# A two-layer recurrent-memory transformer on one core: the memory value sum in column halves, a shorter memory softmax, and the score scale folded into weight products

## Chip, cores, metric

The kernel runs on one core of one Trainium2 chip. The metric is the device time of one execution in microseconds (us). TensorE (PE) multiplies, with its weight loads shown apart as PEld; VectorE (DVE) and ScalarE (ACT) work on vectors and move results out of PSUM; GpSimd (POOL) copies a little; SyncE (SP) issues transfers.

## What is computed

```python
def A(x, mem0):                       # x: 2048 x 448, mem: 8 x 448, 16 heads of 256
    mem = mem0
    for s in range(64):               # segments of 32 tokens
        h = concat(mem, x[32*s : 32*s+32])            # 40 rows
        q, k, v = h @ Wq, h @ Wk, h @ Wv              # per head
        p = softmax(mask(q @ k.T / 16))               # masked scores are -1e9
        o = (p @ v) @ Wo                              # summed over heads
        mem, out[s] = o[:8], o[8:]                    # memory goes to the next segment
    return out
def B(x):
    return (relu(x @ W_gate) * (x @ W_up)) @ W_down
x = x + A(layernorm(x), mem0); x = x + B(layernorm(x))    # layer 0
x = x + A(layernorm(x), mem0); x = x + B(layernorm(x))    # layer 1, the same weights
```

The memory makes `A` a recurrence: segment s+1 cannot start its scores before the 8 memory rows of segment s are there. The two layers run as a pipeline: layer 1 works four segments behind layer 0, in the same step, so there are 68 steps.

## The kernel before

**Weights.** For each head, `M = Wq Wk^T` and `N = Wv Wo` are formed once at the start (`setup`), so that scores are `h M h^T` and the output is `p (h N)`. Both lie in SBUF in 56 blocks of 128 rows (`NO = 56`), with the last 64 of the 448 rows apart (`M3`).

**A step** (`step`, L1399) handles one segment of each layer. The memory's part comes first and is the recurrence: `t_block` forms `M h` (11 groups, in three blocks, copied out to `TTm` and `TTs`), `s_mem` forms the memory rows' scores and their softmax, `p_t_mem` transposes the probabilities, `u_mem` forms `p h` (copied to `UTm`), `un_mem` multiplies it by `N` and sums over the 56 blocks, `m_t` picks the memory rows and transposes them into the next segment's `hT`, and `m_nat` brings them into `hK` in their natural layout. `s_seg`, `seg_pt`, `u_seg` (four pieces) and `un` do the same for the 32 token rows and are not on the recurrence. `ln_b`, `b_layer` and `b_down` are layer B for two segments at a time.

**The order.** No loop sets the order of the instructions. A planner (`_Order.run`, L388) places all operations, engine by engine, by priorities. The priority of a TensorE group is its due time in the table `SLOT`, whose names end in the step modulo 4, so that the order repeats every four steps; the first and last four steps have entries of their own. `BIAS` shifts the priorities of the operations on other engines; its entry `stay` favours a group that needs no new tiling, and `win` sets how far ahead the planner looks. An operation that may run on ACT or DVE (`cp`, L859) goes where the planner expects it to end first. What comes out is a fixed order on each engine, with semaphore waits between engines.

**TensorE's tilings.** Matmuls use the whole 128\*128 array, or four tiles of 64\*64 side by side, or four tiles of 128 rows by 32 columns. `un_mem` uses the last: four quarters of the 56 blocks run side by side, each with the same 32 rows of `UTm` (of both layers) and all 448 columns, and leave four partial sums on the four quarters of PSUM's partitions.

**The sum of the quarters.** In steps 4 to 63 (`stacked`), ACT copies the lower half of the partitions to `sumA` (L1177), DVE adds the upper half into `sumB` (L1178), ACT rounds it to bf16 in the upper half of `hi` (L1179), and DVE writes the rest, again in bf16, into its lower half (L1180). `m_t` and `m_nat` then multiply `hi` by a constant selection matrix (`selm`, `seln`), which adds all rows that belong together. In the other steps `hi` and `lo` are two whole tiles (L1182, L1183), and `m_t` and `m_nat` run over both.

**The memory softmax** (L1070 to L1076): DVE takes the maximum, DVE subtracts it, ACT takes the exponential with the scale 1/16, DVE sums the rows, DVE takes the reciprocal, DVE multiplies. The scores of both layers lie side by side, 40 columns each.

Of the kernel before, what the change touches and what calls it, by code (L numbers as in the profile page):

```python
# [7 lines left out]
F32 = dt.float32  # L8
# [15 lines left out]
NO = 56  # L24
SCALE = 1.0 / 16.0
NEG = -1.6e10
# [18 lines left out]
class _Sched:  # L45
# [118 lines left out]
    "t_blockm+": -2572, "t_blocks+": 1814, "s_mem+": -72176, "p_t_mem+": -4403, "u_mem+": 20875, "un_mem+": -547,  # L164
    "un_memh+": -38848, "m_t+": 9355, "m_tk+": 2366, "s_seg+": 16120, "seg_pt+": 3438, "u_seg0+": -16088,
    "u_seg1+": -717, "u_seg2+": 13160, "u_seg3+": -691, "m_nat+": 82793, "t_block0f+": 12092, "t_block0r+": 515,
    "t_block1r+": -532, "t_block2r+": -10266, "ln_a+": -5223, "ln_ac+": 1567, "un+": 139105, "ln_b+": -4368,
    "b_layer+": 350, "b_down+": 117514, "stay": 11757, "win": 172,
# [5 lines left out]
    "t_block0f.0@a0": 64557, "t_block0r.0@a0": 48742, "t_block0r.1@a0": 66297, "t_block0r.2@a0": 48724,  # L174
    "t_block0r.3@a0": 47759, "t_block0r.4@a0": 48126, "t_block0r.5@a0": 48733, "t_block1f.0@a0": 45822,
    "t_block1r.0@a0": 82085, "t_block1r.1@a0": 94319, "t_block1r.2@a0": 78536, "t_block1r.3@a0": 97965,
    "t_block2r.0@a0": 94795, "s_mem.0@a0": 47753, "fills_mem.0@a0": 56612, "fills_mem.1@a0": 79507,
    "p_t_mem.0@a0": 82024, "u_mem.0@a0": 84238, "fillu_mem.0@a0": 101473, "un_mem.0@a0": 94797, "m_t.0@a0": 96319,
    "s_seg.0@a0": 93758, "u_seg0.0@a0": 85662, "u_seg1.0@a0": 93046, "u_seg2.0@a0": 84258, "u_seg3.0@a0": 93059,
    "m_nat.0@a1": 102575, "t_block0f.0@a1": 47148, "t_block0r.0@a1": 50336, "t_block0r.1@a1": 50332,  # L180
    "t_block0r.2@a1": 50330, "t_block0r.3@a1": 50334, "t_block0r.4@a1": 50338, "t_block0r.5@a1": 50328,
    "t_block1f.0@a1": 47763, "t_block1r.0@a1": 81935, "t_block1r.1@a1": 93766, "t_block1r.2@a1": 93762,
    "t_block1r.3@a1": 93760, "t_block2r.0@a1": 93764, "s_mem.0@a1": 53687, "fills_mem.0@a1": 53691,
    "fills_mem.1@a1": 50369, "p_t_mem.0@a1": 52961, "u_mem.0@a1": 93157, "fillu_mem.0@a1": 66292,
    "un_mem.0@a1": 95431, "m_t.0@a1": 38530, "s_seg.0@a1": 53689, "u_seg0.0@a1": 93038, "u_seg1.0@a1": 93040,
    "u_seg2.0@a1": 93746, "u_seg3.0@a1": 93044, "un0.0@a1": 126022, "un0.1@a1": 126024, "un0.2@a1": 108479,
    "un0.3@a1": 108070, "un1.0@a1": 109020, "un1.1@a1": 103707, "un1.2@a1": 102591, "un1.3@a1": 126036,
    "un2.0@a1": 125114, "un2.1@a1": 126311, "un2.2@a1": 128901, "un2.3@a1": 126313, "un3.0@a1": 126315,
    "un3.1@a1": 126319, "b_layerf.0@a1": 99747, "b_layer.0@a1": 101458, "b_layer.1@a1": 101460,
    "b_layerf.1@a1": 101451, "b_layer.2@a1": 101464, "b_layer.3@a1": 101524, "b_down.0@a1": 101526,  # L190
    "b_down.1@a1": 101468, "b_down.2@a1": 101460, "b_down.3@a1": 101543, "b_down.4@a1": 100495, "b_down.5@a1": 101459,
    "b_down.6@a1": 101539, "m_nat.0@a2": 81979, "t_block0f.0@a2": 47146, "t_block0r.0@a2": 50203,
    "t_block0r.1@a2": 50211, "t_block0r.2@a2": 50986, "t_block0r.3@a2": 50213, "t_block0r.4@a2": 50205,
    "t_block0r.5@a2": 102340, "t_block1f.0@a2": 47162, "t_block1r.0@a2": 102255, "t_block1r.1@a2": 101373,
    "t_block1r.2@a2": 102257, "t_block1r.3@a2": 103206, "t_block2r.0@a2": 50207, "s_mem.0@a2": 59668,
    "p_t_mem.0@a2": 50201, "u_mem.0@a2": 49539, "un_mem.0@a2": 126026, "m_t.0@a2": 126317, "s_seg.0@a2": 122371,
    "u_seg0.0@a2": 113514, "u_seg1.0@a2": 101453, "u_seg2.0@a2": 101528, "u_seg3.0@a2": 101526, "m_nat.0@a3": 126321,
    "t_block0f.0@a3": 49554, "t_block0r.0@a3": 51471, "t_block0r.1@a3": 59670, "t_block0r.2@a3": 59445,
    "t_block0r.3@a3": 50305, "t_block0r.4@a3": 59668, "t_block0r.5@a3": 53676, "t_block1f.0@a3": 49552,
    "t_block1r.0@a3": 100508, "t_block1r.1@a3": 102247, "t_block1r.2@a3": 57648, "t_block1r.3@a3": 101523,  # L200
    "t_block2r.0@a3": 101638, "s_mem.0@a3": 100835, "p_t_mem.0@a3": 101462, "u_mem.0@a3": 100431,
    "un_mem.0@a3": 102605, "m_t.0@a3": 102609, "s_seg.0@a3": 108012, "u_seg0.0@a3": 102306, "u_seg1.0@a3": 102308,
    "u_seg2.0@a3": 102312, "u_seg3.0@a3": 102310, "un0.0@a3": 102607, "un0.1@a3": 107006, "un0.2@a3": 101455,
    "un0.3@a3": 100684, "un1.0@a3": 128108, "un1.1@a3": 101462, "un1.2@a3": 101527, "un1.3@a3": 101529,
    "un2.0@a3": 101531, "un2.1@a3": 101533, "un2.2@a3": 102308, "un2.3@a3": 102310, "un3.0@a3": 102312,
    "un3.1@a3": 102314, "b_layerf.0@a3": 110205, "b_layer.0@a3": 102298, "b_layer.1@a3": 102300,
    "b_layerf.1@a3": 134704, "b_layer.2@a3": 102093, "b_layer.3@a3": 102302, "b_down.0@a3": 101528,
    "b_down.1@a3": 101530, "b_down.2@a3": 101532, "b_down.3@a3": 128003, "b_down.4@a3": 125876, "b_down.5@a3": 106989,
    "b_down.6@a3": 101460, "m_nat.0@0": 136794, "t_block0f.0@0": 58621, "t_block0r.0@0": -19774,
    "t_block0r.1@0": 1609, "t_block0r.2@0": -19782, "t_block0r.3@0": -19780, "t_block0r.4@0": -19778,  # L210
    "t_block0r.5@0": -19776, "t_block1f.0@0": 43923, "t_block1r.0@0": -26408, "t_block1r.1@0": -26410,
    "t_block1r.2@0": -26406, "t_block1r.3@0": -26404, "t_block2r.0@0": 59598, "s_mem.0@0": -32879,
    "p_t_mem.0@0": -19990, "u_mem.0@0": -22021, "un_mem.0@0": -32867, "m_t.0@0": -214033, "s_seg.0@0": 76854,
    "u_seg0.0@0": -22167, "u_seg1.0@0": 43918, "u_seg2.0@0": 319270, "u_seg3.0@0": -23555, "m_nat.0@1": -115912,
    "t_block0f.0@1": -24982, "t_block0r.0@1": -32859, "t_block0r.1@1": -32863, "t_block0r.2@1": -32861,
    "t_block0r.3@1": -32857, "t_block0r.4@1": -20205, "t_block0r.5@1": -32865, "t_block1f.0@1": -23529,
    "t_block1r.0@1": 53151, "t_block1r.1@1": -32851, "t_block1r.2@1": -32853, "t_block1r.3@1": 53153,
    "t_block2r.0@1": -25980, "s_mem.0@1": 53134, "p_t_mem.0@1": 53139, "u_mem.0@1": 61163, "un_mem.0@1": 233375,
    "m_t.0@1": 151657, "s_seg.0@1": 53145, "u_seg0.0@1": 147020, "u_seg1.0@1": 147022, "u_seg2.0@1": 179549,
    "u_seg3.0@1": 147024, "un0.0@1": 147166, "un0.1@1": 62233, "un0.2@1": -23765, "un0.3@1": 65649, "un1.0@1": 61020,  # L220
    "un1.1@1": 237653, "un1.2@1": 151655, "un1.3@1": 237659, "un2.0@1": 237654, "un2.1@1": 151661, "un2.2@1": 151663,
    "un2.3@1": 151638, "un3.0@1": 144006, "un3.1@1": 148365, "b_layerf.0@1": 129357, "b_layer.0@1": 318027,
    "b_layer.1@1": 67000, "b_layerf.1@1": 215789, "b_layer.2@1": 145588, "b_layer.3@1": 61456, "b_down.0@1": -24827,
    "b_down.1@1": -33972, "b_down.2@1": 319243, "b_down.3@1": 319245, "b_down.4@1": 147237, "b_down.5@1": 61345,
    "b_down.6@1": 239065, "m_nat.0@2": 402948, "t_block0f.0@2": 388846, "t_block0r.0@2": 59139,
    "t_block0r.1@2": -26865, "t_block0r.2@2": -26863, "t_block0r.3@2": -26927, "t_block0r.4@2": 145141,
    "t_block0r.5@2": -26869, "t_block1f.0@2": 179407, "t_block1r.0@2": 293702, "t_block1r.1@2": 311085,
    "t_block1r.2@2": 311131, "t_block1r.3@2": 311131, "t_block2r.0@2": 225148, "s_mem.0@2": -30419,
    "p_t_mem.0@2": 59349, "u_mem.0@2": 179549, "un_mem.0@2": -28407, "m_t.0@2": -115541, "s_seg.0@2": 153276,
    "u_seg0.0@2": 318226, "u_seg1.0@2": 317538, "u_seg2.0@2": 232221, "u_seg3.0@2": 146407, "m_nat.0@3": 141188,  # L230
    "t_block0f.0@3": 60228, "t_block0r.0@3": 141563, "t_block0r.1@3": 55559, "t_block0r.2@3": 55561,
# [301 lines left out]
class _Kernel:  # L533
# [16 lines left out]
    def alloc(self):  # L550
# [33 lines left out]
        self.PTm = self.sb("PTm", [128, 128])  # L584

        self.UTm = self.sb("UTm", [128, NO, 64])
        self.hi = self.sb("hi", [128, D])
        self.lo = self.sb("lo", [128, D])
        self.sumA = self.sb("sumA", [64, D], F32)
        self.sumB = self.sb("sumB", [64, D], F32)  # L590
# [871 lines left out]
```

## Time and profile before

| | |
|---|---|
| median of three runs | 1541.28 us (1539.87 to 1543.81) |
| profiled execution | 1540.8 us |
| ACT, DVE busy | 57%, 60% of the span |
| `sumA` copy, ACT, 64 x 448 | 60 of 540 ns |
| `sumB` add, DVE, 64 x 448 | 60 of 614 ns |
| `hi` rounding, ACT | 60 of 575 ns |
| `hi` rest, DVE | 60 of 702 ns |
| softmax maximum, subtraction, sum (DVE, 128 x 80) | 60 each of 238, 241, 231 ns |
| softmax exponential (ACT, 128 x 80) | 60 of 269 ns |

How to read it: the page lists busy times by engine, then the chain of work that ended last, then groups of instructions. A group's row has its line, engine and operation, what it writes and reads, the tile of the array (128\*32), the shape, the number of instructions, their busy time in us and mean in ns, and, after the bar, the idle time of the engine just before them and who ended it. A row of the timeline has the start in us, the duration in us, the engine, the operation, and how many instructions were merged. All matmuls have the line L138, that of a helper, so they are told apart by their tiles: `Nw,UTm` is `un_mem`, `selm` is `m_t`, `seln` is `m_nat`, `PTm,hK` is `u_mem`, `PTs,hK` is `u_seg`, `ident,Pm` is `p_t_mem`, `hT,M` and `hT,Mw` are `t_block`, `Nw,big` is `un`, `xBT,big` and `big,hB` are layer B.

### The profile page before, as it was taken

What the parts mean: (1) busy time and instruction counts of PE and PEld (TensorE: products, weight loads), DVE (VectorE), ACT (ScalarE), POOL (GpSimd) and SP (SyncE); (2) the same over time, 40 slices, a digit from 0 to 9 for tenths busy, and PEclk for the clock granted to TensorE, in tenths of its full rate; (3) what the DMA queues carried; (4) which work ended last, traced back from release to release, by engine and by line L of the source; (5) the groups of instructions that cost most, each with busy time, mean ns of one, the idle gap of its engine ahead of it and who ended that gap; (6) DMA issues with size and microseconds to landing.
All of it is one profiled execution on the core that took longest, in us unless ns stands there. A gap on an engine that the chain in (4) does not pass through costs nothing.

```text
span 1540.8 us, 79677 instructions
## 1 busy us (share of the span) xinstructions
PE 1478.4 (96%) x36772; PEld 1084.9 (70%) x36777; DVE 919.9 (60%) x2445; ACT 882.9 (57%) x2627; POOL 111.8 (7%) x259
## 2 busy tenths in 40 slices
PE   5999989999999999999999999999999999999998
PEld 2567666777676776777677777767677677767675
DVE  7555556656565656655665665656565665566555
ACT  5635555656656565565656565565566566565543
POOL 4000000000000000000000000000000000000000
PEclk9999999999999999999999999999999999999999
DMA  9840100000000000000000010000000010000000
GB/s 224 184 129 16 22 10 20 20 15 17 20 20 15 21 16 19 16 16 20 16 20 15 22 18 15 17 20 20 15 21 16 20 19 16 15 15 19 18 19 14
DMA packets 129726, 45.86 MB, mean 30 GB/s; under 512 B 117736, under 2 KB 129264, under 8 KB 129392
## 3 DMA queue, kind: packets, MB, share of 16 engines
q1 hardware_dynamic: 129040, 40.53, 12.3%
q8 instruction: 288, 4.72, 1.3%
q14 instruction: 46, 0.38, 0.1%
q10 hardware_dynamic: 352, 0.24, 0.1%
HBM read 10.33 MB, written 1.84 MB: 8 GB/s over the span
## 4 chain that ended last, share of the span: by engine, by line
PE 87%; DVE 6%; ACT 4%; DMA 2%; issue 1%; POOL 0%; POOLq 0%
PE b L138 87%; DMA xBT<-xn 2%; ACT UTm L865 2%; DVE big L866 1%; DVE hi L1180 1%; DVE sumB L1178 1%; ACT sumA L865 1%; ACT Mw L865 1%; ACT hi L865 1%; DMA big<-in_A_Wo_dram 0%; DVE xn L919 0%; DVE selm L725 0%; DVE seln L728 0%; DVE stat L912 0%; ACT M L865 0%
## 5 line engine op out<-in xcount | busy, mean ns | idle before, releaser
L138 PE MATMUL b<-hT,Mw 128*128 128x80 bf16 (+1 forms) x11424 | 435.9, 200 | 0.8 <-DVE hT L866 0.7
L138 PEld LDWEIGHTS b<-hT,Mw 128*128 128x128 bf16 x11424 | 417.0, 100 | 12.6 <-DVE hT L866 1.9
L138 PE MATMUL b<-Nw,big 128*32 128x448 bf16 (+1 forms) x3504 | 298.3, 353 | 1.3 <-DVE big L866 0.3
L865 ACT ACTIVATE TTs<-b 128x320 bf16<-128x320 f32 (+4 forms) x649 | 272.6, 422 | 0.7 <-PE b L138 0.6
L865 ACT ACTIVATE TTm<-b 128x80 bf16<-128x80 f32 (+4 forms) x649 | 150.2, 234 | 166.8 <-PE b L138 162.0
L138 PE MATMUL b<-Nw,UTm 128*32 128x448 bf16 x3752 | 193.8, 358 | 19.1 <-ACT UTm L865 17.0
L138 PEld LDWEIGHTS b<-Nw,big 128*32 128x32 bf16 (+1 forms) x3504 | 132.1, 97 | 109.4 <-DVE big L866 7.4
L138 PE MATMUL b<-xBT,big 128*128 128x128 bf16 (+3 forms) x4900 | 205.0, 214 | 3.9 <-issue 2.4
L138 PEld LDWEIGHTS b<-xBT,big 128*128 128x128 bf16 (+1 forms) x4900 | 183.9, 101 | 21.7 <-issue 9.7
L866 DVE CAST TTm<-b 64x64 bf16<-64x64 f32 (+3 forms) x235 | 52.0, 222 | 232.1 <-PE b L138 226.6
L138 PEld LDWEIGHTS b<-Nw,UTm 128*32 128x32 bf16 x3752 | 96.3, 98 | 106.0 <-ACT UTm L865 27.3
L865 ACT ACTIVATE big<-b 128x512 bf16<-128x512 f32 (+1 forms) x228 | 115.6, 557 | 60.3 <-PE b L138 59.9
L138 PE MATMUL b<-hT,M 64*64 64x80 bf16 (+2 forms) x6808 | 142.8, 199 | 2.2 <-ACT M L865 1.0
L138 PEld LDWEIGHTS b<-hT,M 64*64 64x64 bf16 (+2 forms) x6808 | 110.8, 107 | 22.2 <-issue 7.6
L866 POOL COPY hK<-xn 32x448 bf16<-32x448 bf16 x136 | 75.1, 552 | 583.5 <-DVE xn L919 577.2
L865 ACT ACTIVATE UTm<-b 128x512 bf16<-128x512 f32 (+2 forms) x159 | 82.7, 551 | 43.4 <-PE b L138 42.6
L866 DVE CAST big<-b 128x512 bf16<-128x512 f32 (+1 forms) x160 | 93.0, 597 | 11.2 <-PE b L138 10.6
L866 DVE CAST TTs<-b 64x256 bf16<-64x256 f32 (+3 forms) x235 | 97.2, 414 | 0.1
L138 PE MATMUL b<-big,hB 128*32 128x448 bf16 (+1 forms) x742 | 96.6, 353 | 0.0
L1359 ACT ACTIVATE gT<-b 128x512 bf16<-128x512 f32 (+2 forms) x128 | 67.5, 541 | 43.7 <-PE b L138 42.6
L865 ACT ACTIVATE sumA<-b 64x448 f32<-64x448 f32 x60 | 32.4, 540 | 101.6 <-PE b L138 101.6
L138 PE MATMUL b<-PTs,hK 40*64 40x512 bf16 (+1 forms) x1024 | 81.8, 362 | 6.3 <-DVE big L866 5.1
(116 smaller groups left out, 1576.9 us busy)
## 6 DMA issues: line engine op xcount, KB each, us to landing
big<-in_A_Wo_dram SPq DMA_DIRECT2D x3, 896.0 KB, 5.8
out_dram<-ys SPq DMA_DIRECT2D x32, 56.0 KB, 1.9
big<-in_B_W_up_dram SPq DMA_DIRECT2D x7, 224.0 KB, 2.7
big<-in_B_W_gate_dram SPq DMA_DIRECT2D x7, 224.0 KB, 3.5
big<-in_B_W_down_dram SPq DMA_DIRECT2D x7, 224.0 KB, 3.5
XA<-in_A_x_dram SPq DMA_DIRECT2D x28, 56.0 KB, 2.2
PTs<-Ps SPq DMA_TRANSPOSE x67, 2.5
Nw<-in_A_Wo_dram SPq DMA_DIRECT2D x1, 896.0 KB, 5.8
```

What stands on the lines that cost most here:

```text
L138: ins = E.matmul(out, lhsT=lhsT, rhs=rhs, **kw)
L865: return E.activation(out(), src(), ACT.Copy)
L866: return E.tensor_copy(out(), src())
L1178: S.dve(lambda E: E.tensor_tensor(S.sumB[:, :], C.b()[0:64, 0:D], S.sumA[:, :], ALU.add), D, C.res(half=(0,)) + [("sumA",)], [("sumB",)])
L1180: S.dve(lambda E: E.tensor_tensor(S.hi[64:128, :], S.sumB[:, :], S.hi[0:64, :], ALU.subtract), D, [("sumB",), ("hi",)], [("lo",)], base=(0 ...
L1359: S.act(lambda E, g=g, R=R, n=n: E.activation(S.gT[:, g, 0:n], R[0].b()[:, 0:n], ACT.Relu), n, R[0].res(), [("gT", g)])
```

## The change

- **Value sum.** The four tiles of `un_mem` no longer take four quarters of the 56 blocks, but two halves of the blocks by two halves of the columns (`DH = 224`). Each tile then sums 28 blocks over 224 columns, so that only two partial sums remain to be added, each 224 wide.
- **Memory.** ACT copies the lower half (`sumA`), DVE adds and writes bf16 memory rows `mv`. The second bf16 part that carried the rounding error is dropped, and so is the separate path of the first and last steps. `m_t` picks 32 columns at a time in the 128\*32 tiling (14 small matmuls), `m_nat` runs once for each column half.
- **Memory softmax.** The maximum is taken negated and given to the exponential as its bias, one exponential for each layer; the exponential also gives the row sums. DVE's subtraction and sum go.
- **Scale.** The 1/16 goes into `M` when it is copied out of PSUM in `setup`, so the exponentials need none, and the mask constant becomes -1e9.
- **Order.** `SLOT` and `BIAS` have other numbers.

```diff
-    "b_layer+": 350, "b_down+": 117514, "stay": 11757, "win": 172,
+    "b_layer+": -12996, "b_down+": -5101, "m_natx+": -272, "stay": 46, "win": 118,
...
-        S.dve(lambda E: E.tensor_reduce(st[:, 32:32 + nl], src(), AX.X, ALU.max), n, C.res(), [("sm", 0)])
-        S.dve(lambda E: E.tensor_tensor(Em, src(), bc(32), ALU.subtract), n, C.res() + [("sm", 0)], [("Em",)])
-        S.act(lambda E: E.activation(Em, Em, ACT.Exp, scale=SCALE), n, [], [("Em",)], 38.0)
-        S.dve(lambda E: E.tensor_reduce(st[:, 34:34 + nl], Em, AX.X, ALU.add), n, [("Em",)], [("sm", 1)])
+        S.dve(lambda E: E.tensor_reduce(st[:, 32:32 + nl], src(), AX.X, ALU.max, negate=True), n, C.res(), [("sm", 0)])
+        for i in range(nl):
+            S.act(lambda E, i=i: E.activation(S.Em[:, i, :], src()[:, i, :], ACT.Exp, bias=st[:, 32 + i:33 + i], scale=1.0, accum_out=st[:, 34 + i:35 + i]),
+                  KEYS, C.res() + [("sm", 0)], [("Em", i), ("sm", 1, i)], 60.0)
...
-            for k in range(14):
+            for k in range(NO // 2):
                 for j in range(4):
-                    o = 14 * j + k
-                    out.append(MM(C.b()[32 * j:32 * j + 32, 0:D], S.UTm[:, o, 32 * w:32 * w + 32], S.N[:, o, :], start=(k == 0), stop=(k == 13)))
+                    o, d = NO // 2 * (j // 2) + k, DH * (j % 2)
+                    out.append(MM(C.b()[32 * j:32 * j + 32, 0:DH], S.UTm[:, o, 32 * w:32 * w + 32], S.N[:, o, d:d + DH], start=(k == 0), stop=(k == NO // 2 - 1)))
...
-            S.cp(lambda: S.sumA[:, :], lambda: C.b()[64:128, 0:D], D, C.res(half=(1,)), [("sumA",)], eng=("act",), base=(64, 0))
-            S.dve(lambda E: E.tensor_tensor(S.sumB[:, :], C.b()[0:64, 0:D], S.sumA[:, :], ALU.add), D, C.res(half=(0,)) + [("sumA",)], [("sumB",)])
-            S.cp(lambda: S.hi[0:64, :], lambda: S.sumB[:, :], D, [("sumB",)], [("hi",)], eng=("act",))
-            S.dve(lambda E: E.tensor_tensor(S.hi[64:128, :], S.sumB[:, :], S.hi[0:64, :], ALU.subtract), D, [("sumB",), ("hi",)], [("lo",)], base=(0, 64))
+        S.cp(lambda: S.sumA[:, :], lambda: C.b()[64:128, 0:DH], DH, C.res(half=(1,)), [("sumA",)], eng=("act",), base=(64, 0))
+        S.dve(lambda E: E.tensor_tensor(S.mv[0:64, :], C.b()[0:64, 0:DH], S.sumA[:, :], ALU.add), DH, C.res(half=(0,)) + [("sumA",)], [("mem",)])
...
-        S.mm(lambda: [MM(C.b()[:, c * 16:c * 16 + 16], x[:, w:w + 128], S.selm[:, S.win(t), :], start=(i == 0), stop=(i == len(xs) - 1))
-                      for c, w in ((0, 0), (1, 128), (2, 256), (3, 320)) for i, x in enumerate(xs)], 112.0 * len(xs),
-             [("hi",), ("lo",)] + sel, C.res() + mk, alt=2)
+        S.mm(mms, 112.0, [("mem",), ("sel", 0), ("sel", 1)], C.res() + mk, mode=2)
...
-        S.mm(lambda: [MM(C.b()[:, 0:D], S.seln[:, w, :], x[:, :], start=(i == 0), stop=(i == len(xs) - 1)) for i, x in enumerate(xs)],
+        S.mm(lambda: [MM(C.b()[:, DH * j:DH * j + DH], S.seln[:, j, w, :], S.mv[:, :], start=True, stop=True) for j in range(2)],
```

## Prediction

> **What bounds the kernel now.** I read the page first (shares, the chain of waits, the groups), then the timeline of one period of four steps, then the timeline of the first eight steps.
>
> ```profile
> PE 1478.4 (96%) x36772; PEld 1084.9 (70%) x36777; DVE 919.9 (60%) x2445; ACT 882.9 (57%) x2627; POOL 111.8 (7%) x259
> ...
> PE 87%; DVE 6%; ACT 4%; DMA 2%; issue 1%; POOL 0%; POOLq 0%
> ...
> L138 PE MATMUL b<-Nw,UTm 128*32 128x448 bf16 x3752 | 193.8, 358 | 19.1 <-ACT UTm L865 17.0
> ```
>
> TensorE is the bound: 96% busy and 87% of the chain of waits. The last row is the memory value sum (`un_mem`), 56 matmuls in each of 67 steps; most of TensorE's idle time that the page can see stands before it. So DVE or ACT time that is saved is worth nothing by itself. It counts only where TensorE waits for its result.
>
> Busy time hides short waits, because a matmul's tail covers them. So I priced TensorE's order from start times. A matmul of N columns starts N/2.4 + 2.6 ns after the one before it (35.9 ns at 80 columns, 189 at 448; never under 25). In the 64\*64 and 128\*32 tilings four go in that time. A change of tiling adds 95 ns. For the four steps 32 to 35, from one `m_t` to the fourth after it, the order as built gives 80.56 us of matmuls and 42 changes: 80.56 + 42 x 0.095 = 84.55 us. The trace takes 87.9 us (mean from 218.9 to 1449.4 us, 14 periods). So **3.3 us of a period are neither**: 0.9 is about thirty gaps of 24 to 31 ns around 64\*64 groups, and 2.5 are waits. Nearly all of the 2.5 is in the fourth step:
>
> ```profile
> 825.51 0.41 PE L138 MATMUL b<-PTs,hK 40*64 40x512 bf16 x4
> 825.75 0.37 PE L138 MATMUL b<-PTm,hK 40*64 40x128 bf16 x16
> ...
> 825.97 1.52 ACT L865 ACTIVATE UTm<-b 128x512 bf16<-128x512 f32 x3 [0.46 <-PE b L138]
> ...
> 827.54 2.83 PE L138 MATMUL b<-Nw,UTm 128*32 128x448 bf16 x56 [1.21 <-ACT UTm L865]
> ...
> 830.30 0.84 PE L138 MATMUL b<-PTs,hK 40*64 40x512 bf16 x12
> ...
> 830.43 0.54 ACT L865 ACTIVATE sumA<-b 64x448 f32<-64x448 f32 x1 [0.85 <-PE b L138]
> ...
> 831.51 0.30 PE L138 MATMUL b<-PTs,hK 40*64 40x256 bf16 x4 [0.37 <-DVE big L866]
> ```
>
> `un_mem` waits 1.29 us (beyond the tiling change) for a UTm copy that stands third on ACT, behind two segment copies; the last `u_seg` piece waits 0.54 for a bank. The small ones: 0.22 in `un`, 0.14 for xBT, 0.12 before the transpose of Pm, 0.2 elsewhere.
>
> The memory chain after `un_mem`, in a step where other work hides it:
>
> ```profile
> 810.41 0.93 PE L138 MATMUL b<-big,hB 128*32 128x448 bf16 x16
> ...
> 810.63 0.54 ACT L865 ACTIVATE sumA<-b 64x448 f32<-64x448 f32 x1 [1.51 <-PE b L138]
> 811.20 0.62 DVE L1178 TENSOR_TENSOR sumB<-b,sumA 64x448 f32<-64x448 f32 x1 [0.80 <-ACT sumA L865]
> ...
> 811.85 0.58 ACT L865 ACTIVATE hi<-sumB 64x448 bf16<-64x448 f32 x1 [0.68 <-DVE sumB L1178]
> 812.46 0.62 DVE L1180 TENSOR_TENSOR hi<-sumB,hi 64x448 bf16<-64x448 f32 x1 [0.64 <-ACT hi L865]
> ...
> 813.14 0.26 PE L138 MATMUL b<-selm,hi 128*128 128x16 bf16 x4
> ```
>
> From the end of `un_mem` (810.41) to `m_t` (813.14) are 2.73 us. They cost nothing here, since feed-forward matmuls fill them. In the first steps there is too little to fill with:
>
> ```profile
> 161.62 0.23 PE L138 MATMUL b<-ident,Pm 128*128 128x128 bf16 x1 [1.30 <-DVE Pm L1076]
> 162.21 0.59 PE L138 MATMUL b<-PTm,hK 40*64 40x128 bf16 x16 [0.37 <-ACT PTm L865]
> 163.68 5.42 PE L138 MATMUL b<-Nw,UTm 128*32 128x448 bf16 x56 [0.88 <-DVE UTm L866]
> ...
> 194.57 0.27 PE L138 MATMUL b<-selm,hi 128*32 128x16 bf16 x16 [1.36 <-DVE hi L1180]
> ```
>
> After those gaps the granted clock falls: `un_mem` takes 5.42 us instead of 2.83.
>
> **What the Trainium skill says.** (1) "TensorE: Matmul & The Clock Gate", "Wait — 56ns, not 53.3ns?": a warm matmul follows its predecessor by N/2.4 GHz + about 2.5 ns, never under 25. The trace agrees (189 ns at 448). (2) The same page, "What's actually happening": idle time of the array halves its clock. The trace agrees: the window 156 to 176 us has a mean clock of 0.83. (3) "TensorEngine Tiling (Array Packing)", "Key Properties": changing the tiling mode drains the engine. The trace prices it: `un_mem` to the next group takes 2.66 us where the tiling stays (807.75 to 810.41) and 2.76 where it changes (827.54 to 830.30).
>
> **The change, part by part.**
>
> *Value sum.* 56 matmuls of 448 columns become 112 of 224: 14 x 189.3 = 2.65 us become 28 x 95.9 = 2.69, that is +0.04 a step, 67 x 0.036 = +2.4 us. The trace has no 32-column weight load under 224 columns. Lower bound: 64\*64 quads with 64-column loads go at 36 ns for four, and the quartered `m_t` (32-column loads) at 25, so loads don't limit; I take this. Upper bound: the clock-gate page prices a load at columns/1.2, about 27 ns; four in series would be 107 ns for 96, or 28 x 11 ns x 67 = +21 us.
>
> *Memory chain.* Four operations become two of half width: sumA 0.34 (between the 256-column copy, 0.37, and 0.54 at 448) and the add 0.38 (between 0.41 at 256 and 0.61). With the gaps seen above: 0.22 + 0.34 + 0.03 + 0.38 + 0.06 = 1.03 us instead of 2.73. Where the two-part path ran (first and last steps), 1.49 becomes 1.03.
>
> *m_t and m_nat.* 14 small matmuls in 128\*32 and two halves for one: `m_t` 7.4 to 5.9 us in all, `m_nat` 14.0 to 12.9, so -2.7. All matmul time together: 1365.7 to 1365.5 us, nothing.
>
> *Memory softmax.* DVE loses the subtraction (0.24) and the sum (0.23). ACT gets two biased exponentials for one of 0.27. The trace shows none; "ScalarE: Activation LUTs", "What ACT_TABLE_LOAD costs", prices one at 280 + 0.83 x 40 = 313 ns with an overlap of 93 between two; the biased Ln of one column here takes 299. I take 0.57 (bounds 0.45 and 0.66). From the maximum to the transpose, 1.81 us become about 1.56. Only -0.25, hidden by `b_layer`, `un` and `b_down` matmuls in the steady steps.
>
> *Scale.* Folded into copies that run once, on the same engines and sizes, while the load of weights and the products set the pace: 0.
>
> *Order.* The table of due times changes with it, and the order as built has **875 tiling changes instead of 744**: 131 x 0.095 = +12.4 us. In the period 42 become 51: 80.67 + 51 x 0.095 = 85.51, **+0.96**. The 24 to 31 ns gaps stay 0.9. Now the waits. In the fourth step `u_mem` is followed at once by `un_mem`; ACT has one segment copy ahead of UTm instead of two, so UTm is there 1.54 us after the `u_seg` group (825.51 to 827.05 in the trace above), while TensorE is free after 0.22 + 0.02 + 0.20 + 0.13 = 0.56: wait 0.98. Then only two `u_seg` pieces, 0.67 us with the changes of tiling, stand ahead of `m_t`, which needs 1.05: wait 0.38. The bank wait of 0.54 goes, as `m_t` now holds TensorE while the copies finish. For the transpose of Pm I count 0.2, since the segment softmax's maximum (0.49) slips in ahead of the last product; for xBT, `un` and `s_seg` 0.14, 0.1, 0.08. Sum 1.9 for 2.5. Period: 85.5 + 0.9 + 1.9 = 88.3, **+0.43**. Steps 9 to 63 are 13.75 periods: **+5.9 us**.
>
> *First steps.* Up to step 8 the order costs 1.7 us less (190.97 to 189.28). Waits: `m_t` of steps 0 and 1, -1.2; transposes of Pm in steps 5 and 7, -1.1; `m_t` of step 6, 1.6 to 0.1, -1.5; the slow clock after it (196 to 200 us), -2.0; bank waits of 0.8 and 1.1 replaced by short waits of `m_t`, -1.4. Together **-8.9**. *End:* order +1.7, waits -1.1: **+0.6**.
>
> Sum: -8.9 + 5.9 + 0.6 = -2.4; 1541.3 becomes about **1539**.
>
> **The rivals.** *A, no measurable change*, as summed: 1539. *B, faster*: the shorter chain keeps the clock whole in steps 5 and 7 as well (-4 more), other waits of the first steps go (-2), and the period has only the two waits that I can't argue away (0.98 + 0.38 = 1.36), so 87.8, +0 us: -15 + 0.6, **1527 to 1536**, middle 1532. For it: the recurrence is 1.7 + 0.25 us a step shorter. Against it: in the steady period that time was hidden already. *C, slower*: waits in the new period as large as the old ones (2.5), since its `m_t` stands closer to `un_mem` and ACT takes more of the copies; then +0.98 x 13.75 = 13.5, with -5 in the first steps: **1550**. For it: nine more changes a period are certain. Inside C, with a chance of 0.03, weight loads limit: 1560.
>
> **How the numbers follow.** A 0.37, B 0.36, C 0.27. The likeliest gives 1539. The range reaches to B's middle and beyond it, and to C: 1526 to 1552. The chances of faster, same and slower are those of B, A and C.
>
> **What would show it.** Right: `un_mem` groups of 112 take about 2.69 us to the next group; sumA near 0.34 and one add near 0.38; `m_t` 1.05 us after `un_mem`'s end in the fourth step; a period near 88.3; clock whole around 196 us. Wrong: quads of `un_mem` over 100 ns (weight loads), a period under 87.8 (waits went that I count), or waits in the t_block groups or for banks that I did not foresee.

## The result and the profile after

| | before | changed |
|---|---|---|
| median of the runs, us | 1541.88 (1539.87 to 1543.81) | 1547.15 (1546.58 to 1548.94) |
| ratio, 95% interval | 1 | 1.0036 (1.0019 to 1.0054) |
| profiled execution, us | 1540.8 | 1547.1 |

A second measurement of the changed kernel, on another chip beside other kernels, gave 1.0051 (1.0033 to 1.0070). So the change makes the kernel slower by about 0.4%, some 6 us. The forecast was 2.4 us faster; the measured time lies between its limits of 1526 and 1552, but on the slower side of the kernel before.

The page of the changed kernel has its busy times, its chain of waits and two rows of its groups (busy us, mean ns of one, then the idle time ahead of them):

```profile
PE 1489.5 (96%) x40831; PEld 1173.4 (76%) x40835; DVE 826.2 (53%) x2213; ACT 865.0 (56%) x2780; POOL 111.8 (7%) x259
...
PE 86%; ACT 4%; DVE 4%; DMA 3%; SPq 3%; issue 1%
...
L139 PE MATMUL b<-Nw,UTm 128*32 128x224 bf16 x7504 | 196.2, 262 | 17.2 <-DVE UTm L868 15.8
...
L867 ACT ACTIVATE sumA<-b 64x224 f32<-64x224 f32 x67 | 23.7, 354 | 122.0 <-PE b L139 122.0
```

VectorE gave up 94 us of busy time (919.9 before, 826.2 now) and the kernel is slower all the same: that engine was not the bound. The busy time of `un_mem` hardly moved (193.8 before, 196.2 now): the 112 weight loads that it now has a step do not limit it. The chain is still TensorE's (86% for 87%); SyncE's queue (SPq, 3%) is in it by the transposing loads of weights in the setup.

The fourth step of a period, from the timeline (start, duration, engine, operation; in brackets the idle time ahead of it and what ended it):

```profile
920.68 2.87 PE L139 MATMUL b<-Nw,UTm 128*32 128x224 bf16 x112 [1.03 <-DVE UTm L868]
923.59 0.35 ACT L867 ACTIVATE sumA<-b 64x224 f32<-64x224 f32 x1 [0.23 <-PE b L139]
923.98 0.38 DVE L1179 TENSOR_TENSOR mv<-b,sumA 64x224 bf16<-64x224 f32 x1
...
924.07 0.63 PE L139 MATMUL b<-PTs,hK 40*64 40x512 bf16 x8 [0.53 <-DMA PTs<-Ps]
...
924.63 0.27 PE L139 MATMUL b<-selm,mv 128*32 128x16 bf16 x14
```

`m_t` starts 924.63 - (920.68 + 2.87) = 1.08 us after the end of `un_mem` (1.05 forecast). So the memory chain did what it was meant to do.

Where the time went, from the starts of `m_t` in the two timelines, with the priced work (matmuls and tiling changes) and the rest, which is waits and slow clock:

| stretch | before | after | difference | of it priced work | of it waits and slow clock |
|---|---|---|---|---|---|
| start to `m_t` of step 0 | 77.5 | 78.5 | +1.0 | +0.3 | +0.7 |
| steps 0 to 8 | 161.0 | 158.8 | -2.2 | -2.0 | -0.2 |
| steps 8 to 63 | 1210.9 | 1217.1 | +6.2 | +12.2 | -6.0 |
| the rest | 91.4 | 92.7 | +1.3 | | |

The steady stretch came out as forecast (+5.9 forecast, +6.2 found). The first steps did not: -8.9 was forecast up to step 8, and -1.2 was found. There the experiments were aimed. These are single traces: in the trace of the second measurement the three differences against the same trace of before are -3.4 up to step 8, +6.7 and, for the rest, +3.9.

### The profile page after: what moved, and what is told of

Its sections match the earlier page's. It is cut to its first block, busy times and chain, and to the rows that moved or that the text cites. A ratio compares the mean times of both kernels' runs of the same rounds, so it can differ in the third digit from the quotient of the medians.

```text
span 1547.1 us, 87788 instructions
## 1 busy us (share of the span) xinstructions
PE 1489.5 (96%) x40831; PEld 1173.4 (76%) x40835; DVE 826.2 (53%) x2213; ACT 865.0 (56%) x2780; POOL 111.8 (7%) x259
## 4 chain that ended last, share of the span: by engine, by line
PE 86%; ACT 4%; DVE 4%; DMA 3%; SPq 3%; issue 1%
PE b L139 86%; SPq L688 3%; DMA PTs<-Ps 2%; ACT TTs L867 1%; ACT UTm L867 1%; ACT Em L1072 1%; ACT big L867 1%; DMA xBT<-xn 1%; DVE stat L1116 1%; ACT TTm L867 0%; ACT Es L1115 0%; DMA Nw<-in_A_Wo_dram 0%; DVE UTm L868 0%; DVE Es L1114 0%; DVE xn L921 0%
## 5 line engine op out<-in xcount | busy, mean ns | idle before, releaser
L867 ACT ACTIVATE TTs<-b 128x320 bf16<-128x320 f32 (+5 forms) x676 | 282.1, 418 | 22.1 <-PE b L139 20.5
L867 ACT ACTIVATE TTm<-b 128x80 bf16<-128x80 f32 (+5 forms) x660 | 152.7, 232 | 181.6 <-PE b L139 175.8
L139 PE MATMUL b<-Nw,UTm 128*32 128x224 bf16 x7504 | 196.2, 262 | 17.2 <-DVE UTm L868 15.8
L139 PEld LDWEIGHTS b<-Nw,UTm 128*32 128x32 bf16 x7504 | 177.9, 98 | 35.7 <-DVE UTm L868 18.0
L867 ACT ACTIVATE big<-b 128x512 bf16<-128x512 f32 (+1 forms) x250 | 125.4, 559 | 85.5 <-PE b L139 84.5
L868 DVE CAST TTm<-b 64x64 bf16<-64x64 f32 (+4 forms) x224 | 49.7, 223 | 176.0 <-PE b L139 172.6
L868 DVE CAST TTs<-b 64x256 bf16<-64x256 f32 (+5 forms) x208 | 88.9, 428 | 20.0 <-PE b L139 19.8
L1351 DVE TENSOR_TENSOR hB<-gT,b 128x512 bf16<-128x512 bf16 (+2 forms) x128 | 78.3, 614 | 28.3 <-PE b L139 14.4
L867 ACT ACTIVATE UTm<-b 128x448 bf16<-128x448 f32 (+2 forms) x132 | 73.3, 566 | 33.8 <-PE b L139 33.8
L867 ACT ACTIVATE sumA<-b 64x224 f32<-64x224 f32 x67 | 23.7, 354 | 122.0 <-PE b L139 122.0
```

The source lines that it names most:

```text
L139: ins = E.matmul(out, lhsT=lhsT, rhs=rhs, **kw)
L867: return E.activation(out(), src(), ACT.Copy, **({} if scale is None else {"scale": scale}))
L868: return E.tensor_copy(out(), src()) if scale is None else E.tensor_scalar(out(), src(), scale, None, op0=ALU.mult)
L1351: S.dve(lambda E, g=g, R=R, n=n, fcs=fcs: E.tensor_tensor(S.hB[:, fcs[0]:fcs[-1] + 1, 0:w], S.gT[:, g, 0:n].rearrange("p (a b) -> p a b", ...
```

## The experiments

The order of a kernel depends on a table of due times, so a small edit moves hundreds of groups. Therefore in all experiments the planner was replaced by a stored list, which names for each operation its place, engine, tiling and bank:

```diff
     def run(self):
         self.graph()
-        free = {e: 0.0 for e in self.ENGS}
...
+        for i, e, mode, bases, fin in json.loads(zlib.decompress(base64.b85decode(_ORDER_LIST))):
+            o = self.ops[i]
+            o.fixed, o.fin = ("act", "dve", "pe", "pool", "sp")[e], float(fin)
...
+            self.order.append(o)
```

The list holds the planner's own order, so that only the edit named differs: in the run below that moves one transfer, the trace has VectorE's, ScalarE's and GpSimd's sequences of the changed kernel unaltered. An operation that only one kernel has takes the place of its counterpart. (Line numbers of these kernels are shifted by the list.) Ratios are to the kernel before on the same chip.

**Arithmetic and order apart.** The two kernels differ in arithmetic and in order; two runs cross them.

```diff
 # new arithmetic, old order
-_ORDER_LIST = order of the changed kernel
+_ORDER_LIST = order of the kernel before
```

> The changed arithmetic (value sum, softmax, scale) replayed in the order of the kernel before: the same sequence of groups on every engine and the same banks. Its m_t must use the 128*32 tiling, which makes 800 tiling changes of 744. Theory O (the loss comes from the changed order, the new arithmetic is good): shorter memory chain saves 6 to 8 us of waits in the first steps, 56 more tiling changes cost 5.3, so 1538 to 1543. Theory A (the new arithmetic is itself dearer, by its accumulator reads and its 112 small matmuls): 1547 or more.

Measured: 1555.74 us, a ratio of 1.0064 (1.0047 to 1.0082). Theory O falls: the new arithmetic in the old order is no gain. The time is in theory A's range; which part of the arithmetic costs it is narrowed down below. In its trace the waits from step 8 to 63 are 48.1 us, where before has 46.6, and the priced work is 6.8 us more, mostly by 55 more tiling changes around `m_t`. The old order had hidden the memory chain already, so that shortening it freed nothing there. In step 2 a transposing transfer (xBT) also comes 2.9 us late in this trace, as the transpose of Ps does further down.

> The arithmetic of before replayed in the changed kernel's order. Theory O2 (the new order is only bearable because the memory chain is short): the old chain of 2.7 us between un_mem and m_t has 0.7 us of other work in it in every fourth step, so 1.7 us more wait in each of 17 and some elsewhere, 1565 to 1580. Theory A: the old arithmetic is the better one, 1547 or less.

Measured: 1662.83 us, a ratio of 1.0764 (1.0740 to 1.0788). O2's direction is right and its size is far too small. `m_t` in four successive steps of this kernel:

```profile
949.76 0.27 PE L138 MATMUL b<-selm,hi 128*32 128x16 bf16 x16 [0.74 <-DVE hi L1569]
...
973.06 0.26 PE L138 MATMUL b<-selm,hi 128*128 128x16 bf16 x4 [1.36 <-DVE hi L1569]
...
993.57 0.26 PE L138 MATMUL b<-selm,hi 128*128 128x16 bf16 x4 [2.11 <-DVE hi L1569]
...
1017.96 0.27 PE L138 MATMUL b<-selm,hi 128*32 128x16 bf16 x16 [1.42 <-DVE hi L1569]
```

With the old chain `m_t` waits in every step, 5.6 us a period in these lines, and not in the fourth alone. So the new order has used up the slack that the short chain gave. The clock falls again and again in the steady steps of this run as well, which the forecast of 1565 to 1580 did not count. Arithmetic and order belong together, and the pair is 0.4% slower than the old pair.

**The softmax alone**, with the scale part, in the old order, where TensorE's sequence is untouched.

```diff
-        S.dve(lambda E: E.tensor_tensor(Em, src(), bc(32), ALU.subtract), ...)
-        S.act(lambda E: E.activation(Em, Em, ACT.Exp, scale=SCALE), ...)
-        S.dve(lambda E: E.tensor_reduce(st[:, 34:34 + nl], Em, AX.X, ALU.add), ...)
+        for i in range(nl):
+            S.act(lambda E, i=i: E.activation(S.Em[:, i, :], src()[:, i, :], ACT.Exp, bias=..., scale=1.0, accum_out=...), ...)
```

> The softmax part and the scale part alone, on the kernel before in its own order: TensorE's sequence is untouched, the subtraction and the sum leave VectorE, two biased exponentials with accumulated sums replace one on ScalarE. Theory S (two reads of the accumulators make the chain as long as it was): 0.999 to 1.001, with the transposes of Pm waiting 1.3 to 1.7 us in steps 5 and 7 as before. Rival S2 (the forecast's: the chain is 0.25 us shorter, so -0.5 us and no more): also within 0.1%, but with those waits 0.25 shorter. Rival S3 (0.5 us more of ScalarE a step delays UTm and the segment copies): 1.002 to 1.004.

Measured: 1.0000 (0.9987 to 1.0012). The waits of the transposes of Pm in steps 5 and 7 are 1.24 and 1.63 us (1.40 and 1.64 before). S3 falls, and S2 with it, which had both of them 0.25 shorter; theory S fits. So of the 0.64% that the new arithmetic loses in the old order, nothing that can be told comes from softmax and scale. That leaves the value sum with the changes of `m_t` and `m_nat` that go with it; it was not run alone, and the late transfer of step 2 may be part of the loss.

**The sums back on VectorE**, in the changed kernel.

```diff
-  ACT.Exp, bias=st[:, 32 + i:33 + i], scale=1.0, accum_out=st[:, 34 + i:35 + i])
+  ACT.Exp, bias=st[:, 32 + i:33 + i], scale=1.0)
+  S.dve(lambda E: E.tensor_reduce(st[:, 34:34 + nl], S.Em[:, 0:nl, :], AX.X, ALU.add), ...)
```

> The changed kernel with one edit: the biased exponentials without accumulated sums, and one sum over both layers on VectorE ahead of the reciprocal. Theory R (the two reads of the accumulators, 0.2 us each, and the sum on VectorE, 0.23 with 0.06 ahead of it, are worth about the same in the chain, and ScalarE's time is hidden): maximum to Pm within 0.15 us of before the edit, time 1.003 to 1.0055 as without it. Rival (the reads delay UTm and the segment copies in every fourth step): 0.4 us in each of 15 periods, 1.000 to 1.001.

Measured: 1.0072 (1.0059 to 1.0085). Neither time holds: without accumulated sums it is slower by 2.8 us at step 8 and by 8.4 at step 63 (against the second trace of the changed kernel). What theory R said of the chain is right: where nothing comes between, the time from the start of the maximum to the end of Pm goes from 1.41 to 1.50 us. But it took these 0.1 us to be hidden. The groups of the changed kernel (as above: busy us, mean ns of one, idle ahead):

```profile
L1072 ACT ACTIVATE Em<-b,stat 128x40 f32<-128x40 f32 x127 | 36.4, 293 | 22.0 <-DVE stat L1070 21.7
...
L1072 ACT ACTIVATION_READ_ACCUMULATOR Em<-b,stat 128x1 f32 x127 | 25.6, 202 | 0.0
```

With the sums on VectorE:

```profile
L1455 ACT ACTIVATE Em<-b,stat 128x40 f32<-128x40 f32 x127 | 31.0, 294 | 22.7 <-DVE stat L1453 22.3
...
L1457 DVE TENSOR_REDUCE stat<-Em 128x2 f32<-128x80 f32 x60 | 14.0, 233 | 28.1 <-ACT Em L1455 28.1
```

A sum that is taken along is an instruction of its own on ScalarE, 202 ns each; one sum on VectorE for both layers takes 233 ns. With it the transposes of Pm wait 0.1 us more in three of the four steps of a period (0.29 for 0.17, 0.11 and 0.08 for none). In the new order this chain is on TensorE's path at these places, and 0.3 us in each of 13.75 periods are 4.1 of the 5.6 us lost between steps 8 and 63.

**The late transpose of Ps.** The timeline of the changed kernel in step 2, VectorE, SyncE's queue and TensorE:

```profile
105.88 0.33 DVE L1118 TENSOR_TENSOR Ps<-Es,stat 128x160 bf16<-128x160 f32 x1
...
108.68 0.33 SPq L816 DMA_DIRECT2D big<-in_B_W_gate_dram  x1
...
109.05 2.79 SPq L980 DMA_TRANSPOSE PTs<-Ps  x1
...
113.46 0.30 PE L139 MATMUL b<-PTs,hK 40*64 40x256 bf16 x2 [2.77 <-DMA PTs<-Ps]
```

Ps is ready at 106.21, but the queue goes in order: a piece of W_gate stands ahead and waits for its turn until 108.68. Then the transpose takes 2.79 us to issue and TensorE waits 2.77. In the kernel before the same transpose stands ahead of the weight piece, so it is the new order that put it behind:

```profile
104.73 0.32 DVE L1117 TENSOR_TENSOR Ps<-Es,stat 128x160 bf16<-128x160 f32 x1
...
105.09 1.20 SPq L978 DMA_TRANSPOSE PTs<-Ps  x1
...
106.43 0.48 SPq L814 DMA_DIRECT2D big<-in_B_W_gate_dram  x1
```

One edit to the changed kernel moves it back:

```diff
 # SyncE's queue, steps 1 and 2
+seg_pt 2   (transpose of Ps)
 t_block 1  (last piece of W_gate)
-seg_pt 2   (transpose of Ps)
```

> The changed kernel with one DMA moved: on SyncE's queue the transpose of Ps in step 2 stands ahead of the last W_gate piece instead of behind it. Theory P (the transpose was late because the piece ahead of it waits for its turn; the 2.9 us wait of the last u_seg group then halves the clock for 3.4 us): wait and slow window go, 1542 to 1544. Rival (the transfers of weights make the transpose late wherever it stands, or the next wait takes it up): 1546 to 1548.

The timeline of this kernel at the same place:

```profile
106.01 0.33 DVE L1498 TENSOR_TENSOR Ps<-Es,stat 128x160 bf16<-128x160 f32 x1
...
106.36 1.19 SPq L1360 DMA_TRANSPOSE PTs<-Ps  x1
...
107.97 0.33 SPq L1196 DMA_DIRECT2D big<-in_B_W_gate_dram  x1
...
110.67 0.30 PE L139 MATMUL b<-PTs,hK 40*64 40x256 bf16 x2
```

The wait is gone, and `m_t` of step 0 to that of step 3 takes 48.1 us for 52.0 (49.7 in the second trace of the changed kernel). But in all runs the ratio is 1.0041 (1.0027 to 1.0055), no gain that can be told: in this trace 1.8 of the 3.9 us came back between step 3 and step 8, with a slow window in step 7 that is twice as long. The forecast of 1542 to 1544 is missed, and alone the edit is inconclusive for the whole time.

**The slow clock.** Windows of the changed kernel (in each row, after the stretch and its length, busy us and instructions of PE, PEld, DVE, ACT and POOL, then the granted clock, where 0.5 means half, the DMA share and GB/s):

```profile
29.40:33.00 3.60, 3.60 (x14) 1.20 (x11) 1.12 (x5) 2.58 (x6) 0.00 (x0) 0.53 1.07 185
80.60:84.20 3.60, 3.60 (x126) 3.50 (x122) 0.15 (x1) 2.02 (x10) 0.00 (x0) 0.53 0.44 120
114.80:118.40 3.60, 3.60 (x126) 3.50 (x122) 0.95 (x4) 2.01 (x10) 0.00 (x0) 0.53 0.32 85
166.00:173.00 7.00, 5.83 (x120) 4.51 (x124) 1.08 (x3) 0.90 (x2) 0.00 (x0) 0.51 0.11 21
196.20:199.80 3.60, 3.13 (x132) 2.48 (x129) 2.91 (x7) 2.05 (x8) 0.19 (x1) 1.00 0.03 7
210.40:214.00 3.60, 2.79 (x64) 2.46 (x68) 0.76 (x2) 0.18 (x1) 0.00 (x0) 0.53 0.18 36
```

Before has three such windows, 162.2 to 169.2, 196.2 to 199.8 and 210.0 to 213.6. The changed kernel loses the one at 196, as forecast, and has three new ones, at 29, 81 and 115. A window of 3.4 us at half clock can take up to 1.7 us of TensorE's work away: up to 6.8 in sum before, 10.2 after. Fills keep TensorE busy in waits (those of step 0 are left out of the diff):

```diff
     def fill(self, t, n):
-        if t < 2 or t == NSTEP - 1:
+        if t < 2 or t in (5, 7) or t == NSTEP - 1:
...
         S.mm(lambda: [m for c in range(4) ... S.u_mms(l, c, pp, s, ...)], ...)
-        S.fill(t, 1)
+        S.fill(t, 1 if t < 2 else 2)
```

> The changed kernel with idle TensorE time of the first steps filled by matmuls of 512 columns whose result nobody reads: 4 behind un_mem of step 0, 4 ahead of the transpose of Pm and 4 ahead of un_mem in steps 5 and 7. Theory C (part of the missing gain is slow clock after clustered waits): the windows of half clock near 81, 166 to 173 and 210 us go, -6.8, fills overshoot by 0.6: 1540 to 1542. Rival (fills cost what the clock gains, or the clock falls all the same): 1546 to 1549.

Measured: 1.0042 (1.0026 to 1.0058). All the windows that the fills aimed at are gone; two others are left, at 37 and 116. From step 4 to 7 it gains 1.9 us on the first trace of the changed kernel, not 5: `un_mem` is whole again, but part of the slow windows had been waits anyway. The forecast of 1540 to 1542 is missed; the whole time shows nothing, so this too is inconclusive alone.

Both together, and the changed kernel as it is beside it on one chip:

> The changed kernel with both earlier edits: the transpose of Ps of step 2 ahead of the last W_gate piece, and fills in steps 0, 5 and 7. Theory (waits and slow clock of the first steps are what the forecast missed): 4 from the transpose and 2 to 3 from the fills against the changed kernel, so 0.999 to 1.0005 of before. Rival (neither is on the path that sets the end): 1.003 to 1.005.

> The changed kernel as it is, beside the others on one chip: 1.002 to 1.0055. If the 3.2 us wait for a piece of W_k at 28.7 us and the 2.9 us wait for the transpose of Ps at 113.5 us belong to the kernel, both are there again; if they are chance, others stand in their place.

Measured: 1.0021 (1.0013 to 1.0029) with both edits and 1.0051 (1.0033 to 1.0070) without. The intervals do not touch: the two edits together gain 0.3% (3.8 us between the medians 1549.67 and 1545.90, 4.6 by the ratios). That lies between the forecast and its rival, and the kernel is still no faster than before. The repeated kernel has the wait for W_k and the wait for the transpose of Ps again:

```profile
28.51 2.05 PE L139 MATMUL b<-big,Nw 128*128 128x448 bf16 x5 [2.23 <-DMA big<-in_A_Wk_dram]
...
111.12 0.30 PE L139 MATMUL b<-PTs,hK 40*64 40x256 bf16 x2 [1.59 <-DMA PTs<-Ps]
```

It does not have the slow windows at 81 and 115. So the waits belong to the kernel, and where the clock falls after them differs from run to run. With both edits only one slow window is left, at 36. Steps 0 to 8 take 151.9 us, for 158.8 and 156.5 without; `m_t` of step 8 is then 7.6 us ahead of the kernel before, and the steady steps (+7.0) and the end (+1.7) use that up.

The same fills in the kernel before, and ahead of `m_t` of step 6:

> The kernel before with its idle TensorE time in steps 5 to 7 filled by matmuls of 512 columns whose result nobody reads: 4 ahead of the transpose of Pm and 4 ahead of un_mem in steps 5 and 7, 6 ahead of m_t of step 6. Theory C (slow clock after clustered waits costs real time): un_mem and the groups after it get back 2.6 + 0.8 us in step 5, about 1.2 after m_t in step 6, 1.5 in step 7: -5.5, a ratio of 0.996 to 0.997. Rival (what the clock gains comes back as waits for the copies of other engines): 0.999 to 1.001.

Measured: 1537.69 us, 0.9968 (0.9960 to 0.9977). The windows of the kernel before:

```profile
162.20:169.20 7.00, 6.11 (x76) 2.58 (x80) 1.35 (x4) 0.59 (x2) 0.00 (x0) 0.51 0.10 21
196.20:199.80 3.60, 3.60 (x85) 3.39 (x86) 2.90 (x6) 2.39 (x9) 1.92 (x4) 0.53 0.22 42
210.00:213.60 3.60, 3.15 (x36) 1.39 (x40) 0.40 (x1) 0.07 (x1) 0.00 (x0) 0.53 0.18 36
```

With fills:

```profile
162.20:169.20 7.00, 5.53 (x94) 2.44 (x93) 3.00 (x9) 2.53 (x7) 0.00 (x0) 1.00 0.10 21
196.20:199.80 3.60, 3.60 (x142) 3.48 (x143) 1.44 (x3) 2.81 (x11) 2.49 (x5) 1.00 0.19 41
210.00:213.60 3.60, 2.78 (x32) 1.11 (x25) 2.64 (x5) 2.94 (x6) 0.00 (x0) 1.00 0.00 0
```

The clock is whole in all three, and 0.32% is gained: 4.9 us by the ratio, 4.7 between the medians (1542.36 and 1537.69), nearly the 5.5 forecast. Theory C holds, and this version beats both kernels. It also shows that slow clock after waits is not the change's alone: the kernel before has it too. (In the changed kernel the fills alone showed no gain that can be told.)

**VectorE's queue in steps 5 and 7.** Why did the transposes of Pm not come earlier? The timeline of step 5 of the changed kernel, with ScalarE's last read of a sum, VectorE, and the transpose:

```profile
163.34 0.24 ACT L1072 ACTIVATION_READ_ACCUMULATOR Em<-b,stat 128x1 f32 x1
...
163.80 0.48 DVE L1113 TENSOR_REDUCE stat<-b 128x8 f32<-128x320 f32 x1
...
164.19 0.15 DVE L1074 RECIPROCAL stat<-stat 128x2 f32<-128x2 f32 x1
...
164.31 0.49 DVE L1114 TENSOR_TENSOR Es<-b,stat 128x320 f32<-128x320 f32 x1
...
164.72 0.23 DVE L1076 TENSOR_TENSOR Pm<-Em,stat 128x80 bf16<-128x80 f32 x1
...
165.01 0.23 PE L139 MATMUL b<-ident,Pm 128*128 128x128 bf16 x1 [1.23 <-DVE Pm L1076]
```

The sums are there at 163.58, but the reciprocal stands behind the segment softmax's maximum and Pm behind its subtraction. Moving these two (and the segment exponential) back:

```diff
 # VectorE's queue, steps 5 and 7
-s_seg maximum
 s_mem reciprocal
-s_seg subtraction
 s_mem Pm
+s_seg maximum
+s_seg subtraction
```

> The changed kernel with VectorE's and ScalarE's order changed in steps 5 and 7 alone: maximum and subtraction of the segment softmax go behind Pm, its exponential behind the copy of PTm. Theory V (VectorE's queue, not the softmax itself, sets when Pm is there: the reciprocal stands behind the segment maximum, 0.4 us, and Pm behind the segment subtraction, 0.4): the waits of the transposes of Pm, 1.33 and 1.29 us, become 0.5 to 0.65, and the clock may stay whole in one of the two steps: 1.5 to 4 us, a ratio of 1.0015 to 1.004. Rival (the exponentials or the copies ahead of them set it): waits of 1.2 or more, 1.0045 as before the edit.

Measured: 1.0049 (1.0032 to 1.0067), no gain. In step 5:

```profile
165.24 0.23 PE L139 MATMUL b<-ident,Pm 128*128 128x128 bf16 x1 [0.50 <-DVE Pm L1456]
...
167.81 0.62 DVE L1248 CAST UTm<-b 128x448 bf16<-128x448 f32 x1
...
168.48 1.07 PEld L139 LDWEIGHTS b<-Nw,UTm 128*32 128x32 bf16 x28 [1.98 <-DVE UTm L1248]
```

Theory V is right on the wait that it names, less so on its size: 1.33 and 1.29 us (beyond the tiling change) become 0.60 and 0.84, where 0.5 to 0.65 was expected. But the segment softmax now stands ahead of the UTm copy, and `un_mem` waits 2.09 and 2.28 for 1.28. The sum of the three waits in step 5 was 1.33 + 0.45 + 1.28 = 3.06 and is 0.60 + 0.71 + 2.09 = 3.40. The wait changed its place, and the clock falls in both steps as before.

> The best version so far, the kernel before with fills, with the same change of VectorE's order in steps 5 and 7 and half the fill (2 matmuls of 512 for 4) ahead of the transpose of Pm. Theory V: 0.8 us less in each of the two steps on top of the fills, so 0.9955 to 0.996 of before. Rival (with the clock whole, other waits take the time up, as in the joined version): 0.9968 or more, as with fills alone.

Measured: 0.9996 (0.9984 to 1.0007), 0.28% worse than with full fills. Theory V falls here too: `un_mem` waits 1.36 and 1.35 us behind its fill, and in step 5 the clock falls again (173.4 to 176.8). `m_t` of step 4 to that of step 5, and of step 6 to step 7, takes 24.1 and 22.7 us for 21.8 and 21.4 with full fills. Two things were changed at once, so whether the order or the halved fill let the clock fall is not shown; and the trace is of the slowest of the 14 runs (1550.4, median 1543.0), with a further slow stretch in step 3.

**New first steps, old steady steps.**

```diff
     def un_mem(self, t):
         S = self
+        if t >= 8:
+            return S.un_mem_old(t)   # likewise m_t and m_nat
```

> Steps 0 to 7 with the changed kernel's value sum, order, fills and moved transpose, from step 8 on the value sum and the order of before (the softmax of the changed kernel throughout). Theory (the changed kernel gains in the first steps and loses in the steady ones, and the two can be had apart): 79 us to m_t of step 0, 152 to that of step 8, then 1210.5 to step 63 and 92 for the rest: 1533 to 1535, a ratio of 0.994 to 0.9955. Rival (the seam between the two orders, or before's order after new first steps, gives the gain back): 0.997 or more.

Measured: 0.9993 (0.9984 to 1.0002). The theory falls. At `m_t` of step 7 this kernel is 3.6 us ahead of the kernel before with fills, but step 7 to 8 takes 22.5 us for 19.6: the old order finds work there that the new one had put off. (Up to step 7 the priced work is 170.2 us, against 173.5 in the kernel before with fills, so that 3.4 of the 3.6 us were work still to be done.) After step 8 only 0.6 is left. A start of `m_t` says how far the recurrence is, not how much work is done. From step 31 to 63 it loses 2.6 us more: about 1.8 in five pauses inside `s_seg` for which the profile shows no cause, and about 1.0 in waits for the transpose of Ps; why is left open.

## Why the prediction was wrong

- **Value sum**: right. Its quads (four matmuls, one in each tile) follow each other in 96 ns, as priced (95.9); the upper bound, where loads limit, is out.
- **Memory chain**: right. sumA 0.35 and one add 0.38 for 0.34 and 0.38; `m_t` 1.08 us after `un_mem`.
- **Softmax**: too large. Where nothing comes between, the time from the start of the maximum to the end of Pm went from 1.56 to 1.41 us, -0.15 for the -0.25 forecast. Two biased exponentials with their sums end 0.69 us after they begin (162.89 to 163.58); 0.57 were taken, since the read of the accumulator was not counted.
- **Order and steady waits**: right in sum, in part by luck. The order cost 12.2 us from step 8 to 63 where the forecast comes to 13.2 (0.96 x 13.75), and the waits fell by 6.0 where it comes to 7.3; the two misses cancel. The period goes from 1210.9/13.75 = 88.1 to 88.5 us, +0.45 (+0.43 forecast); waits of `un_mem` 1.11 (0.98 forecast), of Pm 0.17 (0.2). The 0.38 forecast for `m_t` in the fourth step is shared: the two values alternate, 0.39, or 0.72 ahead of it for the DMA of PTs. Steps 8 to 63 +6.2 for +5.9 (+6.7 in the second trace).
- **End**: +0.6 forecast, +1.3 found, and +3.9 in the second trace, which has a slow window at 1482 to 1486; not looked into.
- **First steps: the step that failed.** -8.9 was forecast: -1.7 by the order and -7.2 by waits and slow clock. The order gave its -1.7. Waits and slow clock gave +0.5 in its place in the first trace (-1.2 in sum), and in the second trace the sum is -3.4. Of the terms: `m_t` of step 6 was right (its wait went from 1.62 to 0.17), and the clock after it stayed whole as forecast. The bank waits went (0.80 and 0.70 in steps 5 and 7). `m_t` of steps 0 and 1 gave about half of 1.2, since `m_nat` now waits 1.06 in its place. The transposes of Pm gave 0.4 of 1.1, since VectorE's queue, more than the softmax, sets them. And two things stood at nothing: SyncE's queue, where the new order put the transpose of Ps behind a weight piece (2.9 us, and 1.7 in the second trace), and new slow windows (three of up to 1.7 us in the first trace). I counted only windows that would go.

  As a rough sum for the first trace, 0.6 + 0.7 for the two terms that were too large, 2.9 for the transpose and 5.1 for the three windows make 9.3, where 7.7 are missing; waits and slow clock overlap, so it need not come out exactly. In the second trace the slow windows up to step 8 are as long in sum as before (13.7 us), so that only the forecast -2.0 fails to come: 1.3 + 1.7 + 2.0 = 5.0, where 5.5 are missing. The gain by the two edits is no measure of the two missing terms alone, since the fills also mend the windows at 166 and 210, which the kernel before has too.

  `m_t` of step 6 in the changed kernel, with no idle time ahead of it, where the prediction's line has 1.36:

```profile
196.28 0.24 PE L139 MATMUL b<-selm,mv 128*32 128x16 bf16 x12
```

The forecast also called no measurable change likeliest because two terms of unequal certainty cancelled: +5.9 came from fourteen equal periods, -8.9 from eight steps that occur once.

## What to carry to other kernels

A chain that is hidden by other work is worth nothing when it gets shorter; it becomes worth something only if the order is changed to need it, and then the order's price (here nine more tiling changes a period) is to be paid from it. In a start-up stretch, list every queue that a transfer stands in, SyncE's too, and count slow clock after clustered waits as a cost that can come as well as go. And try filling the waits before shortening what they wait for: 22 idle matmuls in five waits of the kernel before gained 0.3%, where the whole change lost 0.4%.

## What the hardware showed that I had not expected

- A sum taken along by an activation appears as a second instruction, ACTIVATION_READ_ACCUMULATOR, 202 ns beside 293 for the exponential itself. It starts 0.18 us after the exponential and overlaps it.
- The windows of half clock are 3.4 or 6.8 us long and come at other places in runs of one kernel (81 and 115 us in one trace, not in the other). The Trainium skill, "TensorE: Matmul & The Clock Gate", "What's actually happening", says that the clock is judged in a free-running window of 3.41 us. The traces agree: within each trace that has several, the starts of the slow windows lie whole multiples of 3.413 us apart, to within 0.003 us. A free-running window would make the places vary so.
- The same section has the clock fall after at least one idle window. Here less is enough. Take the stretches of 3.413 us on that raster, from 20 us on, and add up the streaming time of the matmuls that start in each (N/2.4 ns for N columns, a quarter of it where four tiles run side by side). Ahead of all 55 falls of the clock it is 7 to 43% of the stretch; of 6135 stretches after which the clock stayed whole, nine are as low (34 to 42%). So in this program the clock falls when the array streams for less than about 40% of one such stretch, and several short waits in one stretch do it as well as a long one. Traces lack some matmul records (19 of the 22 idle matmuls of the kernel before with fills are there), so the limit is rough.
- TensorE pauses inside a group although nothing that the profile shows holds it. One such pause is ahead of the last ten matmuls of `un_mem` in the changed kernel with fills:

```profile
153.36 0.47 PE L139 MATMUL b<-Nw,UTm 128*32 128x224 bf16 x10 [0.95 <-issue]
```

  Pauses of over 0.25 us of this kind sum to between 1.4 and 7.7 us in the traces, in most of them mainly in the first 250 us. Their cause was not looked into. They and the waits for weights in the setup (2 to 3 us, different in each trace) are why differences of under 2 us between whole stretches of single traces prove little.
- The transposing transfer of Ps took 1.19 us to issue 1.1 us after a weight piece; right behind one it took 2.79 in the changed kernel and 2.18 in its second trace, but 1.20 in the kernel before with fills and the reordered softmax:

```profile
110.07 0.33 SPq L1206 DMA_DIRECT2D big<-in_B_W_gate_dram  x1
110.44 1.20 SPq L1370 DMA_TRANSPOSE PTs<-Ps  x1
```

  So the place in the queue makes it late, as the moved transfer shows, but does not alone explain how long the issue takes; that stays open.
